# Second norms of blocks 1 and 2 on GpSimd, a 5120-column product, first loads in pieces, and a new order

## The chip, the core and the metric

The kernel runs on one core of a Trainium2 chip. The metric is the device time of one execution in microseconds, and the time of a kernel is the median of several executions. Of the kernel before there are three: 256.29, 257.15 and 257.36 us, median 257.15 us. A further execution was recorded by the hardware profiler; it took 256.16 us, and its span from the first to the last instruction is 254.4 us.

The names of the engines in the profile: PE is TensorE (matmuls, transposes), PEld its weight load, DVE is VectorE, ACT is ScalarE, POOL is GpSimd, SP is the engine that issues most DMAs. A "q" behind a name is the engine's sequencer.

## The reference, cut to what matters

Sequence length 2048, width 640, hidden width 1728, bfloat16. Part A is a gated long convolution: a four-tap shift of `k`, times `v`, convolved over the sequence with a filter as long as the sequence (through a Fourier transform), times the normed query. Part B is a SwiGLU layer behind a second norm.

```
h  = x + A(layernorm(x), k, v, shift_k, ssm_k, ssm_D)
h2 = h + B(layernorm(h), w_gate, w_up, w_down)

A: kv = shift4(k, shift_k) * v
   y  = irfft(rfft(kv, 4096) * rfft(ssm_k, 4096))[:2048] + kv * ssm_D
   return q * y
B: return (silu(x @ w_gate) * (x @ w_up)) @ w_down
```

## The kernel before

The sequence is cut into four blocks of 512 rows (`NB` = 4, `BLK` = 512). A row tile of a block is 128 partitions by four rows `r` by 640 columns. For each block j the work is staged, and the stage names stand in the program:

- `g`: the filter piece `ssm_k` is transposed on PE (line 431) and evicted from PSUM (line 435); block 3 uses DMA transposes instead. In block 0 a row of `ssm_D` is added (line 437).
- `k`: the shifted `k` by small matmuls with the diagonal taps `diag` (line 570, "conv" below), times `v`, gives `kv` (line 578, straight out of PSUM on DVE, or line 579 on ACT and line 580 on DVE). Block 0 first transposes `k` on PE (line 533) into `T` (line 537).
- `G`, `X`: the spectra of `g` and `kv`, matmuls with the basis `WF` (line 352), evicted by line 344 (ACT) or line 345 (DVE), and some sums (lines 377 to 409). In block 0 the spectra and the products are made in two half-widths of 320 columns (`CUTS`).
- `m`: products of spectra, A = sum of X[i] times H[j-i] (function `mac`): the first pair of a block by line 591, the others by lines 612 (product) and 615 (sum into A). A whole-width product has 2560 columns, a half-width one 1280. Function `sum_into` lets a sum go either on DVE or as an accumulating DMA that POOL issues (line 256).
- `n`, `i`: `ln1` takes the sums of x (lines 671 and 628 on ACT) and the first norm; `inverse` forms the inverse transform (DVE lines 697 to 733, PE line 745), multiplies it by the normed query (lines 685 or 682, then line 759), adds x (line 762) and takes the second norm of h.
- `t`: h is scaled (lines 685 or 682) and transposed: in block 0 on PE (line 783, evicted by line 785), in blocks 1 to 3 by DMA transposes (line 776).
- `f`: the SwiGLU layer: line 846 (up and gate, 540 matmuls of 512 columns), lines 835 and 837 (evictions), line 840 (product), lines 915 and 900 (down projection), line 924 (out of PSUM) or lines 933 and 935 (last block).

The FFN of block j is written behind the mixing of block j+1, so that PE can do the one while the other engines prepare the other.

A norm turns four sums per partition into a scale and a bias. On DVE it is `norm`: nine or ten instructions of 128 by 4 elements, with a polynomial for the inverse root (lines 643 to 653). On GpSimd it is `apart`: five instructions with a power (lines 660 to 664). Before the change the first norms of blocks 1 to 3 run in `apart`, everything else in `norm`.

Nothing schedules itself: every step is an operation with an engine, a function and its buffers, and the list `ORDER` of operation numbers says in which order they are issued; a negative number takes the operation's other engine (ACT or DVE for evictions, DVE or a DMA for sums, the SP or the POOL queue for loads). Each engine takes its instructions in that order, so an instruction that waits holds up everything behind it on its engine. Buffers are handed out along the same list: 13 large tiles `big`, eight spectra `S`, five rows `row`, four PSUM tiles `ps` that all PE results share.

PSUM tiles are the tightest: PE may be at most four results ahead of the engines that evict them.

Of the kernel before, what the change touches and what calls it, by code (L numbers as in the profile page):

```python
# [14 lines left out]
ALU = mybir.AluOpType  # L15

S_TOT = 2048
D = 640
FF = 1728
P = 128  # L20
# [18 lines left out]
GPIECES = ((0, KT),)  # L39
# [150 lines left out]
def kernel(ctx: ExitStack, tc: tile.TileContext, A_q, A_k, A_v, A_shift_k, A_ssm_k, A_ssm_D, B_x,  # L190
# [156 lines left out]
    def forward(src, c, rs, ps, ws, first, last, holds):  # L347

        def mm():
            for i, r in enumerate(rs):  # L350
                for h in ws:
                    nc.tensor.matmul(ap(ps)[:, h, 0:NH], ap(WF)[:, c, r, :], ap(src)[:, r, h * NH:(h + 1) * NH],  # L352
                                     start=(first and i == 0), stop=(last and i == len(rs) - 1), skip_group_check=True)
        pe(136 * len(ws) * len(rs), mm, [(src, r) for r in rs] + [WF] + ([] if first else [ps]), [ps], holds)
# [152 lines left out]
    def load_k(j):  # L507

        if j == 0:
            return load_t(kk, 0)  # L510
# [593 lines left out]
```

## Time and profile before

| | value |
|---|---|
| three executions | 256.29, 257.15, 257.36 us; median 257.15 us |
| the profiled execution | 256.16 us, of which the span is 254.4 us |
| DMA traffic | 41.04 MB in 51906 packets, mean 161 GB/s |
| POOL, ACT busy | 67.4 us (27%), 174.9 us (69%) |
| granted TensorE clock, mean | 0.993 |

The page gives busy time by engine, the span in 40 slices with a digit for the busy share of each engine, the chain that ended last, and groups of instructions by source line. Queries of the trace give the same by window, by engine in order of time, and the waits. In a row of the timeline the first number is the start in us from the span's start, the second the length of that row, "xN" the number of instructions merged in it, and the bracket the idle time just before it with what ended it. Instructions that follow each other are pipelined, so a row's busy time per instruction is longer than the step from one start to the next; sums below use the step. The start of a matmul is exact, its end is modelled.

### The profile page before, as it was taken

What the parts mean: (1) busy time and instruction counts of PE and PEld (TensorE: products, weight loads), DVE (VectorE), ACT (ScalarE), POOL (GpSimd) and SP (SyncE); (2) the same over time, 40 slices, a digit from 0 to 9 for tenths busy, and PEclk for the clock granted to TensorE, in tenths of its full rate; (3) what the DMA queues carried; (4) which work ended last, traced back from release to release, by engine and by line L of the source; (5) the groups of instructions that cost most, each with busy time, mean ns of one, the idle gap of its engine ahead of it and who ended that gap; (6) DMA issues with size and microseconds to landing.
All of it is one profiled execution on the core that took longest, in us unless ns stands there. A gap on an engine that the chain in (4) does not pass through costs nothing.

```text
span 254.4 us, 5139 instructions
## 1 busy us (share of the span) xinstructions
PE 246.7 (97%) x2070; PEld 145.2 (57%) x2070; DVE 192.1 (76%) x280; ACT 174.9 (69%) x306; POOL 67.4 (27%) x73
## 2 busy tenths in 40 slices
PE   8699999999999999999999999999999999999994
PEld 7566667744555576645554567544447744444663
DVE  0599999999989999999979999999998300102213
ACT  3969999998679899686788984348668144635200
POOL 6300020113444011149932013136920024000000
PEclk9799999999999999999999999999999999999999
DMA  6999777998897979898976386989973229000011
GB/s 239 350 356 234 196 203 141 211 249 199 159 330 199 176 169 183 205 200 207 278 142 119 83 126 119 187 192 212 211 158 80 58 46 131 0 0 0 3 41 62
DMA packets 51906, 41.04 MB, mean 161 GB/s; under 512 B 25461, under 2 KB 46202, under 8 KB 51882
## 3 DMA queue, kind: packets, MB, share of 16 engines
q1 hardware_dynamic: 45040, 26.94, 41.5%
q0 software_dynamic: 6832, 13.77, 30.5%
q8 instruction: 16, 0.26, 0.4%
q14 instruction: 8, 0.07, 0.1%
q10 hardware_dynamic: 10, 0.01, 0.0%
HBM read 22.03 MB, written 4.59 MB: 105 GB/s over the span
## 4 chain that ended last, share of the span: by engine, by line
PE 86%; ACT 6%; DMA 3%; DVE 2%; issue 1%; SPq 0%; DVEq 0%
PE ps L846 46%; PE ps L915 22%; PE ps L352 7%; ACT S L344 5%; PE ps L745 4%; PE ps L570 4%; DMA big<-in_A_ssm_k_dram 3%; PE ps L431 1%; PE ps L900 1%; DVE big L578 1%; ACT big L435 1%; ACT row L628 1%; DVE S L345 1%; ACT row L685 0%; ACT big L785 0%
## 5 line engine op out<-in xcount | busy, mean ns | idle before, releaser
L846 PE MATMUL ps<-big,big 128*128 128x512 bf16 x540 | 120.6, 379 | 0.0
L846 PEld LDWEIGHTS <-big 128*128 128x128 bf16 x540 | 52.0, 98 | 60.1 <-issue 0.5
L915 PE MATMUL ps<-wd,tT 128*128 128x320 bf16 (+2 forms) x416 | 59.5, 299 | 0.0
L915 PEld LDWEIGHTS <-tT 128*128 128x128 bf16 x416 | 40.3, 98 | 16.8 <-issue 1.3
L352 PE MATMUL ps<-big,WF 128*128 128x320 bf16 x224 | 37.0, 298 | 1.1 <-ACT S L344 0.4
L344 ACT ACTIVATE S<-ps 128x640 bf16<-128x640 f32 (+1 forms) x62 | 33.4, 620 | 4.3 <-PE ps L352 4.0
L612 DVE TENSOR_TENSOR big<-S,S 128x2560 bf16<-128x2560 bf16 x24 | 34.8, 1486 | 0.7 <-DMA S<-big 0.4
L835 ACT CAST co<-ps 128x1024 bf16<-128x1024 f32 x24 | 24.1, 1016 | 15.3 <-PE ps L846 15.1
L837 ACT ACTIVATE tT<-ps 128x1024 bf16<-128x1024 f32 x24 | 24.6, 1024 | 13.8 <-PE ps L846 13.7
L352 PEld LDWEIGHTS <-WF 128*128 128x128 bf16 x224 | 21.4, 97 | 12.7 <-issue 3.2
L628 ACT ACTIVATE row<-big 128x640 bf16<-128x640 bf16 x32 | 23.8, 752 | 2.2 <-DVE big L762 1.2
L840 DVE TENSOR_TENSOR tT<-tT,co 128x2048 bf16<-128x2048 bf16 x12 | 14.7, 1222 | 13.0 <-ACT co L835 9.0
L615 DVE TENSOR_TENSOR S<-S,big 128x2560 bf16<-128x2560 bf16 x16 | 23.4, 1486 | 0.1
L256 POOL DMA_DIRECT2D S<-big x9 | 10.9, 1210 | 46.0 <-DVE big L612 14.6
L685 ACT ACTIVATE row<-big,sm 128x640 bf16<-128x640 bf16 x22 | 19.6, 928 | 2.7 <-DVE sm L653 1.7
L858 DVE TENSOR_TENSOR tT<-tT,co 128x512 bf16<-128x512 bf16 x4 | 1.7, 422 | 21.7 <-ACT tT L856 21.3
L925 POOL DMA_DIRECT2D out_dram<-row x12 | 12.1, 1314 | 17.3 <-ACT row L924 17.2
L256 POOL DMA_DIRECT2D S<-S x4 | 5.7, 1431 | 38.2 <-ACT S L344 38.2
L924 ACT CAST row<-ps 128x640 bf16<-128x640 f32 x12 | 8.1, 690 | 10.3 <-PE ps L900 6.6
L759 DVE SCALAR_TENSOR_TENSOR row<-row,ps 128x640 bf16<-128x640 bf16 x16 | 12.8, 818 | 3.1 <-PE ps L745 2.9
L570 PEld LDWEIGHTS <-T 64*128 64x128 bf16 x640 | 12.0, 113 | 4.2 <-issue 4.0
L570 PE MATMUL ps<-diag,T 64*128 64x64 bf16 x640 | 13.5, 198 | 0.0
(93 smaller groups left out, 276.1 us busy)
## 6 DMA issues: line engine op xcount, KB each, us to landing
S<-big POOLq DMA_DIRECT2D x9, 640.0 KB, 6.3
big<-in_B_w_gate_dram SPq DMA_DIRECT2D x11, 320.0 KB, 5.6
big<-in_B_w_up_dram SPq DMA_DIRECT2D x10, 320.0 KB, 6.6
big<-in_A_q_dram SPq DMA_DIRECT2D x4, 640.0 KB, 5.5
big<-in_A_ssm_k_dram SPq DMA_DIRECT2D x4, 640.0 KB, 7.0
big<-in_A_v_dram SPq DMA_DIRECT2D x4, 640.0 KB, 4.3
S<-S POOLq DMA_DIRECT2D x4, 640.0 KB, 6.8
wd<-in_B_w_down_dram SPq DMA_DIRECT2D x1, 2080.0 KB, 12.2
```

Of the source, the lines that this page charges most:

```text
L256: nc.gpsimd.dma_start(out=to(), in_=what(), accum_op=ALU.add, max_dma_last_dim=2 * D * 2)
L344: plan.add("act", 700 if n else 430, lambda: nc.scalar.activation(dst(), src(), ACT.Copy, scale=by), [ps], [part], (), ("dve", 820 if n el ...
L352: nc.tensor.matmul(ap(ps)[:, h, 0:NH], ap(WF)[:, c, r, :], ap(src)[:, r, h * NH:(h + 1) * NH], start=(first and i == 0), stop=(last and i ...
L570: nc.tensor.matmul(out()[:, b, c, :], k, ap(diag)[at, c, t, :], start=(t == 0), stop=(t == 3))
L612: dve(1490, lambda b=b, xs=xs, hs=hs: nc.vector.tensor_mul(flat2(b), X.part(xs), H.part(hs)), [X.at(xs), H.at(hs)], [b], [A.b])
L615: f(A.part(dst), A.part(dst), flat2(b))
L628: act(825, lambda r=r, junk=junk: nc.scalar.activation(ap(junk), ap(x)[:, r, :], ACT.Square, scale=D ** -0.5, accum_out=sm(s, 1)[:, r:r + ...
L685: nc.scalar.activation(ap(row), ap(x)[:, r, :], ACT.Identity, bias=sm(s, 5)[:, r:r + 1], scale=sm(s, 4)[:, r:r + 1])
L835: act(1010, lambda ps=ps: nc.scalar.copy(ap(co)[:, at:at + 2, :], ap(ps)), src, [(co, gi % 2)])
L837: act(1010, lambda ps=ps: nc.scalar.activation(ap(tT)[:, c:c + 2, :], ap(ps), ACT.Silu), src, [done(range(c, c + 2), ROWS)])
L846: nc.tensor.matmul(ap(ps)[:, i, :], ap(w)[:, k, off:off + P], ap(hT)[:, k, :], start=(k == 0), stop=(k == KT - 1))
L915: nc.tensor.matmul(ap(ps)[:, hf, 0:n], ap(tT)[:, c, at:at + P], ap(wd)[:, c, col:col + n], start=j % 2 == 0 and c == order[0], stop=j % 2 ...
```

## The change

Five things change in the text of the program.

1. The second norms of blocks 1 and 2 (`FAR`) go to `apart` on GpSimd, which gains two instructions for the mean: seven instead of ten on DVE.
2. In `mac`, the first two products of a block, X's first half with both halves of H, become one instruction of 5120 columns: X's half is read twice (a broadcast) and H in turned order. Only whole-width products do so, in blocks 1, 2 and 3; block 0 keeps half-widths.
3. The first loads of `k` and `v` come in two halves each, `WF` in two halves, the first filter piece in two pieces (two and three of five 128-row groups).
4. The matmuls of a spectrum wait for their half of `WF`, the transposes for their piece of the filter.
5. `ORDER` is new throughout. With it some sums change engine: 11 instead of 13 large and 4 instead of 6 small sums are accumulating DMAs, the rest are on DVE. Ahead of the first FFN matmul PE has 148 instead of 160 matmuls of line 352; the total is the same.

```diff
@@ constants
-GPIECES = ((0, KT),)
+FAR = (1, 2)
+GPIECES = ((0, 2), (2, KT))
...
 ORDER = [
-    0, 4, 2, 15, 1, 16, 5, 6, 19, 22, 20, 24, 26, 17, 18, 3, 23, 344, 9, 7, -26, -11, 28, -15, 353, 44, 29, 12, 200, 13,
+    0, 15, 1, 16, 2, 9, 4, 17, 5, 3, 6, 23, 22, 7, 24, 26, 21, 19, 28, 11, 14, 32, 20, -14, 29, 30, -34, -11, -32, 12, 18,
...
@@ forward
-        pe(136 * len(ws) * len(rs), mm, [(src, r) for r in rs] + [WF] + ([] if first else [ps]), [ps], holds)
+        pe(136 * len(ws) * len(rs), mm, [(src, r) for r in rs] + [(WF, c // 2)] + ([] if first else [ps]), [ps], holds)
...
@@ class Spec
+        def turns(self, swapped=False):
+            t = ap(self.b).rearrange("p a (s b) d -> p a s (b d)", s=2)
+            return t if self.swapped == swapped else t[:, :, ::-1, :]
+
+        def twice(self, sin):
+            t = self.part(sin)
+            return t.unsqueeze(2).broadcast_to([P, 2, 2, 2 * D])
...
@@ load_k
-            return load_t(kk, 0)
+            return load_t(kk, 0, 2)
...
@@ mac
-            dve(n, op(v.tensor_mul, of(A, 0), of(X, 0), of(H, 0)), [x0, H.at(0, ws)], [A.at(0, ws)])
-            dve(n, op(v.tensor_mul, of(A, 1), of(X, 0), of(H, 1)), [x0, H.at(1, ws)], [A.at(1, ws)])
+            if len(ws) == 2:
+                dve(2820, op(v.tensor_mul, lambda: A.turns(H.swapped), lambda: X.twice(0), lambda: H.turns(H.swapped)),
+                    [x0, H.at(0), H.at(1)], [A.at(0), A.at(1)])
+            else:
+                dve(n, op(v.tensor_mul, of(A, 0), of(X, 0), of(H, 0)), [x0, H.at(0, ws)], [A.at(0, ws)])
+                dve(n, op(v.tensor_mul, of(A, 1), of(X, 0), of(H, 1)), [x0, H.at(1, ws)], [A.at(1, ws)])
...
@@ apart
-    def apart(s):
+    def apart(s, mean=None, rs=range(R)):
...
         def go():
+            if mean:
+                v.tensor_scalar(sm(s, 2), sm(s, 0), -1.0 / D, None, op0=ALU.mult)
+                v.tensor_add(sm(s, 2), sm(s, 2), sm(mean, 2))
...
-        plan.add("pool", 5500, go, [root], [s])
+        plan.add("pool", 7000 if mean else 5500, go, [root] + ([mean] if mean else []), [s])
...
@@ inverse
-            norm(s, n1, rs)
+            (apart if plan.block in FAR else norm)(s, n1, rs)
...
@@ first loads
-    v = load_t(vv, 0)
+    v = load_t(vv, 0, 2)
...
-    load(P * R * 4 * P * 2, 4096, lambda: nc.sync.dma_start(out=ap(WF), in_=wf_h.ap()), [WF])
+    for c in (0, 2):
+        load(P * R * 2 * P * 2, 2048, lambda c=c: nc.sync.dma_start(out=ap(WF)[:, c:c + 2], in_=wf_h.ap()[:, c:c + 2]), [(WF, c // 2)])
```

The new program's lines stand 1 to 17 further down; where both are named, the line of before comes first: conv 570/579, transposes of g 431/432, forward 352/353, its evictions 344/345 and 345/346, kv 578/587, the second norm's DVE instructions 643/656 and up, FFN 846/862.

**First place: the loads and PE's first real work.** On SP, the queue of the loads at the program's start, before (big_72 is `k`, big_73 the query x, big_74 the filter piece g, big_75 `v`):

```order
L317 DMA big_72<-in_A_k_dram 128x2560
L323 DMA big_73<-in_A_q_dram 128x2560
L309 DMA big_74<-in_A_ssm_k_dram 128x5x512
L317 DMA big_75<-in_A_v_dram 128x2560
L987 DMA WF<-const_wf 128x2048
L807 DMA big_76<-in_B_w_up_dram 128x5x256
```

And the same stretch of SP's queue after the change:

```order
L318 DMA big_72<-in_A_k_dram 128x1280 x2
L324 DMA big_73<-in_A_q_dram 128x2560
L310 DMA big_74<-in_A_ssm_k_dram 128x3x512
L310 DMA big_74<-in_A_ssm_k_dram 128x2x512
L1004 DMA WF<-const_wf 128x1024
L318 DMA big_75<-in_A_v_dram 128x1280
L1004 DMA WF<-const_wf 128x1024
L318 DMA big_75<-in_A_v_dram 128x1280
```

The same bytes go in the same order as far as g; behind it the halves of `WF` and `v` take turns, and the FFN weights that came next have moved back. On PE, the transposes of `k` (line 533/542) end and the following work begins; before, the transposes of g come first:

```order
L533 MATMUL ps_96<-ident,big_72 128x128
L431 LDWEIGHTS big_74
L431 MATMUL ps_94<-ident,big_74 128x128
...
L570 LDWEIGHTS T
L570 MATMUL ps_93<-diag,T 128x64
```

After, the first 40 matmuls of the conv stand there, and g's transposes (line 432) behind them:

```order
L542 LDWEIGHTS big_72
L542 MATMUL ps_94<-ident,big_72 128x128
L579 LDWEIGHTS T
L579 MATMUL ps_93<-diag,T 128x64
...
L432 LDWEIGHTS big_74
```

So PE's first work behind the transposes of `k` no longer needs g, but needs `T`, which is made from those transposes, and the taps `diag`.

**Second place: DVE ahead of block 1's spectrum.** The second norm of block 0 (sm_99) stays on DVE in both; `kv` of block 1 (lines 578/587 and 580/589) stands among it. Before:

```order
L643 SCALAR_TENSOR_TENSOR sm_99<-sm_99,sm_98 128x4
L580 TENSOR_TENSOR big_72<-big_72,big_74 128x640
L578 TENSOR_TENSOR big_72<-ps_93,big_74 128x2x5x64
L578 TENSOR_TENSOR big_72<-ps_94,big_74 128x2x5x64
L645 TENSOR_TENSOR sm_99<-sm_99 128x4
L435 COPY big_79<-ps_96 128x640
L646 SCALAR_TENSOR_TENSOR sm_99<-sm_99 128x4
```

After:

```order
L656 SCALAR_TENSOR_TENSOR sm_99<-sm_99,sm_98 128x4
L778 TENSOR_TENSOR big_73<-big_73,row_90 128x640
L658 TENSOR_TENSOR sm_99<-sm_99 128x4
L587 TENSOR_TENSOR big_75<-ps_96,big_81 128x2x5x64
L589 TENSOR_TENSOR big_75<-big_75,big_81 128x640
L436 COPY big_79<-ps_93 128x640
L659 SCALAR_TENSOR_TENSOR sm_99<-sm_99 128x4
L660 TENSOR_SCALAR sm_99<-sm_99 128x4
L661 TENSOR_TENSOR sm_99<-sm_99 128x4
L587 TENSOR_TENSOR big_75<-ps_94,big_81 128x2x5x64
L662 SCALAR_TENSOR_TENSOR sm_99<-sm_99 128x4
L589 TENSOR_TENSOR big_75<-big_75,big_81 128x640
```

The last of block 1's four kv rows has moved back behind four more instructions of the norm.

**Third place: POOL and ACT at block 1's second norm (sm_101).** On POOL the seven instructions stand between two accumulating DMAs (line 257, sums of spectra):

```order
L257 DMA S_67<-S_70 128x2x1280
L674 TENSOR_SCALAR sm_101<-sm_101 128x4
L675 TENSOR_TENSOR sm_101<-sm_101,sm_100 128x4
L676 TENSOR_TENSOR sm_101<-sm_101 128x4
L677 TENSOR_TENSOR sm_101<-sm_101 128x4
L678 TENSOR_SCALAR sm_101<-sm_101 128x4
L679 TENSOR_TENSOR sm_101<-sm_101,root 128x4
L680 TENSOR_TENSOR sm_101<-sm_101 128x4
L257 DMA S_71<-big_80 128x2x1280
```

On ACT, which scales h with the result (line 701), a run of evictions stands between the last sum of squares (line 641) and the first row that needs the norm:

```order
L641 ACTIVATE row_87,sm_101<-big_82 128x640
L345 ACTIVATE S_66<-ps_93 128x640
L851 CAST co_92<-ps_95 128x1024
...
L345 ACTIVATE big_83<-ps_93 128x640
L345 ACTIVATE big_83<-ps_95 128x640
L701 ACTIVATE row_90<-big_82,sm_101 128x640
L345 ACTIVATE big_79<-ps_93 128x640
```

Before, DVE made this norm, spread over its other work; now ACT's first scaling waits for POOL, and the evictions behind it wait with it.

78 rows, old and new, of the table ORDER are left out of this document.

## The prediction

> **What bounds the kernel now.** First the page: busy shares, and two rows of its slices (40 equal slices of 6.4 us, a digit is tenths of busy time).
>
> ```profile
> span 254.4 us, 5139 instructions
> PE 246.7 (97%) x2070; PEld 145.2 (57%) x2070; DVE 192.1 (76%) x280; ACT 174.9 (69%) x306; POOL 67.4 (27%) x73
> PE   8699999999999999999999999999999999999994
> DVE  0599999999989999999979999999998300102213
> ```
>
> PE is full from the fourth slice to the last. So other engines matter only where PE waits for them. Next, then, PE's timeline at the front and at the last block's FFN.
>
> ```profile
> 6.51 0.44 PE L533 MATMUL ps<-ident,big 128*128 128x128 bf16 x5 [0.20 <-ACT T L537]
> 8.78 0.52 PE L431 MATMUL ps<-ident,big 128*128 128x128 bf16 x5 [1.83 <-DMA big<-in_A_ssm_k_dram]
> 16.48 0.76 PE L570 MATMUL ps<-diag,T 64*128 64x64 bf16 x40
> 45.19 0.44 PE L783 MATMUL ps<-ident,row 128*128 128x128 bf16 x5
> 45.46 0.71 PE L352 MATMUL ps<-big,WF 128*128 128x320 bf16 x4
> 47.83 4.00 PE L352 MATMUL ps<-big,WF 128*128 128x320 bf16 x28
> 51.72 8.58 PE L846 MATMUL ps<-big,big 128*128 128x512 bf16 x39
> 206.81 29.31 PE L846 MATMUL ps<-big,big 128*128 128x512 bf16 x135
> ```
>
> The only long wait is 1.83 us, for the first filter piece. What I take as the hinge is 51.72, the start of the first FFN matmul: before it PE does what the front's chain allows, behind it PE never waits as long as the others keep up. The rest is 254.4 − 51.72 = 202.7 us of PE work. I therefore forecast the hinge and the rest apart.
>
> **The rest.** Twelve matmuls of line 352 move behind the hinge. Their step is (51.72 − 47.83)/28 = 0.139 us, so the rest becomes 202.7 + 12 × 0.139 = 204.4, if nothing new stalls PE.
>
> **The front, step by step.** DVE carries it. Its rows, with the filter's DMA (from the chain of waits) and POOL's `diag`:
>
> ```profile
> 1.72 7.02 DMA big<-in_A_ssm_k_dram
> 3.78 5.12 POOL L978 TENSOR_SCALAR diag<-row,taps 128x64 bf16<-128x64 bf16 x12 [1.26 <-DVE taps L970]
> 9.34 0.49 DVE L435 COPY big<-ps 128x640 bf16<-128x640 bf16 x1 [1.11 <-PE ps L431]
> 12.65 0.47 DVE L437 TENSOR_TENSOR big<-big,row 1x640 bf16<-1x640 bf16 x1
> 13.05 0.47 DVE L435 COPY big<-ps 128x640 bf16<-128x640 bf16 x1
> 13.45 1.53 DVE L578 TENSOR_TENSOR big<-ps,big 128x640 bf16<-128x640 f32 x2
> 21.13 0.82 DVE L591 TENSOR_TENSOR S<-S,S 128x1280 bf16<-128x1280 bf16 x1
> 40.36 0.16 DVE L643 SCALAR_TENSOR_TENSOR sm<-sm,sm 128x4 f32<-128x4 f32 x1
> 42.30 0.15 DVE L645 TENSOR_TENSOR sm<-sm 128x4 f32<-128x4 f32 x1
> 42.96 0.17 DVE L647 TENSOR_SCALAR sm<-sm 128x4 int32<-128x4 int32 x1
> 44.14 0.16 DVE L653 TENSOR_TENSOR sm<-sm 128x4 f32<-128x4 f32 x1
> 48.85 1.48 DVE L591 TENSOR_TENSOR S<-S,S 128x2560 bf16<-128x2560 bf16 x1
> 50.25 1.48 DVE L591 TENSOR_TENSOR big<-S,S 128x2560 bf16<-128x2560 bf16 x1
> ```
>
> 1. *g lands at the same time.* It came at 1.72 + 7.02 = 8.74. The bytes ahead of it in SP's queue are the same; four issues instead of three stand there. I take 8.75 ± 0.4. Its transposes are no longer PE's first work: the conv runs from about 7.95 (POOL makes eight `diag` pieces, 3.78 + 8 × 5.12/12 = 7.2; DVE's last `T` is ready by 7.8) to 8.7, in what was the idle stretch. First eviction of g on DVE 9.2, before 9.34.
> 2. *Four evictions and the row add follow.* At DVE's step of 13.05 − 12.65 = 0.40 they end at 9.2 + 5 × 0.40 = 11.25; before it was 13.45, since convs stood between the transposes.
> 3. *The clock may fall or not.* The windows (PE busy is the second number, the granted clock the one ahead of the DMA share):
>
> ```profile
> 2.24:5.65 3.41, 3.23 (x34) 2.96 (x32) 0.18 (x1) 0.63 (x2) 2.15 (x6) 1.00 0.93 356
> 5.65:9.07 3.42, 1.39 (x21) 1.10 (x19) 2.14 (x11) 2.78 (x7) 3.25 (x8) 1.00 0.99 326
> 9.07:12.48 3.41, 3.41 (x73) 2.99 (x72) 1.22 (x3) 3.41 (x11) 0.00 (x0) 0.50 1.06 368
> ```
>
>    A window in which PE was busy 1.39 of 3.42 us was followed by one at clock 0.50, one with 3.23 by full clock. After the change the conv fills the middle window to some 55%, between the two. If the clock falls, half of PE's 3.41 us is lost, most of it behind the four PSUM tiles: 0 to 0.5 us on the end. I take 0.3.
> 4. *To the first product.* Before, 21.13 − 13.45 = 7.7. After the change one conv of 0.76 (row at 16.48) and 0.25 of DVE work are left over for it: + 1.0. First product at 11.25 + 7.7 + 1.0 = 19.95, 1.2 earlier.
> 5. *The products and the inverse.* Before 40.36 − 21.13 = 19.2, DVE nearly without a gap. The same 18 half-width instructions stand there; an `h` row (0.40), a kv sum (0.40) and three norm instructions (about 0.5 together) move out, and I add 0.2 of waits: 18.1, so 38.05.
> 6. *To block 1's last kv row.* By the order list after the change: two products straight out of PSUM (half of the 1.53 at 13.45 each), four instructions of 640 columns at 0.40, and six norm instructions at (44.14 − 42.96)/6 = 0.20: 1.5 + 1.6 + 1.2 = 4.3, so 42.35; before, the last row was done at 42.30. Here the lead is given back, because norm instructions now stand ahead of it.
> 7. *From there PE is the limit*: 36 matmuls at 0.139 and 25 transposes at (45.46 − 45.19)/5 = 0.054 are 6.4. Hinge 42.35 + 6.4 + 0.3 (step 3) = 49.05 against 51.72.
>
> Sum: 49.05 + 204.4 = 253.45, 0.95 under 254.4. The profiled execution took 256.16, 1.76 more than its span; the median of the runs, 257.15, lies 0.99 above that. So 253.45 + 1.76 + 0.99 = **256.2 us**.
>
> **The other edits.** *DVE's total*: 20 norm instructions of 0.20 go, 4.0 us. Two large sums at 50.25 − 48.85 = 1.40 and two small ones at 0.40 come back from DMAs, 3.6. DVE gains almost nothing, and PE does not wait for it in the middle anyway.
>
> *The 5120-column product* does not stand in the trace. These groups bound it:
>
> ```profile
> L591 DVE TENSOR_TENSOR S<-S,S 128x2560 bf16<-128x2560 bf16 x6 | 8.9, 1486 | 0.0
> L591 DVE TENSOR_TENSOR S<-S,S 128x1280 bf16<-128x1280 bf16 x4 | 3.2, 821 | 0.0
> L733 DVE TENSOR_TENSOR S<-big 128x1280 bf16<-128x1280 bf16 x6 | 4.7, 818 | 0.0
> ```
>
> The line through 1280 and 2560 columns has 0.52 ns per column, so 5120 take 1486 + 2560 × 0.52 = 2.82 us, against 2 × 1.40 of step: nothing gained. Line 733 reads its operand in turned order at the plain rate, so I take 2.82. The upper end is half rate for a repeated operand, 5.6.
>
> *The second norms on GpSimd.* The trace has first norms there, first and last instruction of each of two:
>
> ```profile
> 66.85 0.50 POOL L660 TENSOR_TENSOR sm<-sm 128x4 f32<-128x4 f32 x1 [5.33 <-ACT row L671]
> 72.46 0.54 POOL L664 TENSOR_TENSOR sm<-sm 128x4 f32<-128x4 f32 x1
> 114.03 7.09 POOL L660 TENSOR_TENSOR sm<-sm 128x4 f32<-128x4 f32 x1 [1.79 <-ACT row L671]
> 124.93 0.21 POOL L664 TENSOR_TENSOR sm<-sm 128x4 f32<-128x4 f32 x1
> ```
>
> Five instructions took 72.46 + 0.54 − 66.85 = 6.15 us and 11.11 us. Seven at those rates are 8.6 to 15.6; the first is the more usual make-up (no single instruction of 7 us in it), and I take 10 to 11. It hides behind ACT's evictions between the last sum of squares and the first scaling of h: nine of them for block 1. In the trace ACT's evictions at that place run at PE's pace:
>
> ```profile
> 81.71 0.70 ACT L344 ACTIVATE S<-ps 128x640 bf16<-128x640 f32 x1
> 94.69 2.20 ACT L344 ACTIVATE big<-ps 128x640 bf16<-128x640 f32 x3
> ```
>
> Eleven of them from 81.71 to 96.9, 1.38 us each; eight such steps are 11 us of cover. So the norm just fits, and costs nothing at 11 us or less. Beyond that ACT's scaling stands at the head of its queue with the evictions behind it, PE has four PSUM tiles, some 1.5 us, and then stops; POOL's accumulating DMAs behind the norm come late too.
>
> Here a rule speaks against the change. One instruction of 128 by 4 elements took 7.09 us while DVE ran two-input instructions without a gap, others about 1.45, DVE's step. The Trainium skill, page "SBUF — State Buffer", section "Who interferes with whom", says that DVE and GpSimd share a pair of ports as an exclusive lock, held for a whole instruction, and that a DVE instruction with two SBUF inputs contends with a GpSimd one that reads SBUF. The trace agrees with these two numbers; by that rule a 5120-column product holds GpSimd off twice as long.
>
> **The rivals.**
> - *The front's whole lead is kept.* The 1.0 in step 4 and some 0.7 of DVE waits in step 5 are guesses from the order list; DVE had gaps of that size before. Without them the hinge is 47.35: 256.2 − 1.7 = **254.5**. Against it: step 6 shows the same norm in DVE's way.
> - *The lead is lost at the last block.* These rows end DVE's and SP's part of block 3:
>
> ```profile
> 198.94 0.16 DVE L653 TENSOR_TENSOR sm<-sm 128x4 f32<-128x4 f32 x1
> 199.49 5.17 SPq L776 DMA_TRANSPOSE big<-row  x4
> ```
>
>   The last transpose is issued at 199.49 + 5.17 = 204.66 and its data is needed at 206.81: about 2 us for the transfer. If PE comes 0.95 us sooner and DVE, whose work is the same within 0.4 us, doesn't, PE waits there for most of it: 256.2 + 0.8 = **257.0**, no change.
> - *Slower: a norm on GpSimd outlasts its cover.* At 15.6 us against 11 the scaling is 4.6 late, less 1.5 that PE holds: 3 us in one block, 256.2 + 3 = **259.2**; in both, 262. It decides from 11 us on. For it speaks the row of 7.09, against it the row at 66.85.
> - *Slower: the 5120-column product at half rate.* 3 × 2.8 = 8.4 us more on DVE, a part of it covered by DVE's 24% of idle time: **260 to 265**. Line 733's row speaks against it.
> - *The change doesn't do what it says*, the conv can't start before g because `diag` or `T` is late: PE idles as before and the time of before stays, **257.2**; I count it with the case of no change.
>
> **How the numbers follow.** The forecast, 256.2, has chance 0.40, own range 255.2 to 257.2; the front's whole lead 0.24; lost at the last block (or not brought) 0.19; the norm late 0.13; half rate 0.04. 0.5%, about what a measurement of this kernel can tell from no change, is 1.29 us: faster means under 255.86. Faster: 0.24 + 0.17 of the forecast's (its range lies across the bound) = 0.41. Same: 0.23 + 0.19 = 0.42. Slower: 0.17. For the range, 253.6 (the kept lead less 0.9) to 259.4 (one late norm and a little) leaves out the half-rate case, the case of two late norms and the tails.
>
> **What would show it.** Right: line 432's first transpose at about 8.75 behind a conv, the first half-width product near 19.95, the last kv row of block 1 near 42.35, the first FFN matmul near 49, PE without a wait behind it; a group of 5120 columns with a mean near 2.82 us; GpSimd's seven instructions in 8.6 to 11 us. Wrong: PE waiting in front of a line 353 or 862 for ACT (a late norm), PE waiting for a DMA at the last block's FFN (lost there), a 5120 row of over 4 us, or g landing later than 9.2, which moves every step behind it.

## The result and the profile after

The changed kernel is slower. Five runs gave 258.44 to 261.66 us, median 260.56, beside a median of 257.36 us for the kernel before (five runs); the ratio is 1.0119, 95% interval 1.0087 to 1.0151. The forecast was 256.2 us, in a range that ended at 259.4. The profiled execution took 258.87 us with a span of 257.2, 2.8 more than the span before. The ratios here and below leave out executions more than 1.5% above the fastest of their kernel, the medians don't, so runs are compared by their ratios, of which 1% is 2.6 us.

These lines of the page answer to those of before: span, busy shares, and PE's and DVE's slices.

```profile
span 257.2 us, 5111 instructions
PE 244.4 (95%) x2053; PEld 145.1 (56%) x2070; DVE 194.6 (76%) x264; ACT 174.4 (68%) x306; POOL 82.0 (32%) x80
PE   8699799999979999999989999999999999999995
DVE  3589999999996999999859999999998500031213
```

PE's row has a 7 in the twelfth slice (70.7 to 77.2 us) and an 8 in the 21st (128.6 to 135), where before it had nines; the 7 in the fifth belongs to the front. So the loss lies in two places behind the front. PE's timeline shows them, and the start of the first FFN matmul above them:

```profile
49.79 7.72 PE L862 MATMUL ps<-big,big 128*128 128x512 bf16 x34
75.56 0.43 PE L353 MATMUL ps<-big,WF 128*128 128x320 bf16 x2 [0.92 <-ACT S L345]
77.28 1.24 PE L862 MATMUL ps<-big,big 128*128 128x512 bf16 x5 [0.74 <-ACT tT L853]
129.21 0.87 PE L579 MATMUL ps<-diag,T 64*128 64x64 bf16 x40 [0.72 <-ACT tT L853]
130.60 0.38 PE L862 MATMUL ps<-big,big 128*128 128x512 bf16 x1 [0.52 <-ACT big L588]
```

The hinge came 1.93 us earlier (51.72 before). The rest is 257.2 − 49.79 = 207.4 us where 204.4 was forecast, 3.0 too much, and the four waits in brackets sum to 0.92 + 0.74 + 0.72 + 0.52 = 2.9. All four are waits for ACT's evictions. ACT's timeline just ahead of each pair says what ACT was doing:

```profile
70.09 1.03 ACT L853 ACTIVATE tT<-ps 128x1024 bf16<-128x1024 f32 x1
73.19 1.73 ACT L701 ACTIVATE row<-big,sm 128x640 bf16<-128x640 bf16 x2 [2.07 <-POOL sm L680]
74.83 0.68 ACT L345 ACTIVATE S<-ps 128x640 bf16<-128x640 f32 x1
123.96 0.70 ACT L588 CAST big<-ps 128x640 bf16<-128x640 f32 x1
127.33 0.92 ACT L701 ACTIVATE row<-big,sm 128x640 bf16<-128x640 bf16 x1 [2.67 <-POOL sm L680]
128.15 1.00 ACT L853 ACTIVATE tT<-ps 128x1024 bf16<-128x1024 f32 x1
```

ACT stood at the first scaling of x (line 701, 685 before) until GpSimd's last norm instruction (line 680), with evictions behind it. This is the **first** norm of blocks 1 and 2, which was on GpSimd before the change too, not the second one that the change moves there. GpSimd's and DVE's timelines in block 1 show why it was late (the two engines apart):

```profile
62.30 5.94 POOL L676 TENSOR_TENSOR sm<-sm 128x4 f32<-128x4 f32 x1 [2.84 <-ACT row L687]
68.31 1.45 POOL L677 TENSOR_TENSOR sm<-sm 128x4 f32<-128x4 f32 x1
72.62 0.54 POOL L680 TENSOR_TENSOR sm<-sm 128x4 f32<-128x4 f32 x1
...
62.08 1.48 DVE L628 TENSOR_TENSOR S<-S,big 128x2560 bf16<-128x2560 bf16 x1
63.48 1.48 DVE L625 TENSOR_TENSOR big<-S,S 128x2560 bf16<-128x2560 bf16 x1
64.89 1.48 DVE L628 TENSOR_TENSOR S<-S,big 128x2560 bf16<-128x2560 bf16 x1
66.29 0.48 DVE L589 TENSOR_TENSOR big<-big,big 128x640 bf16<-128x640 bf16 x1
66.69 1.48 DVE L628 TENSOR_TENSOR S<-S,big 128x2560 bf16<-128x2560 bf16 x1
68.21 1.49 DVE L713 TENSOR_TENSOR big<-S 128x2560 bf16<-128x2560 bf16 x1
```

GpSimd had its sums at 62.30. Its first instruction, 128 by 4 elements, ended at 68.24, just where DVE's stream has its first gap behind 62.30: the sum at 66.69 ends at 68.17, and line 713, which needs that sum, starts at 68.21. The steps before are 1.40 us or 0.40, with each instruction starting before the last one ends. In block 2 the same instruction took 7.73 us:

```profile
115.31 7.73 POOL L676 TENSOR_TENSOR sm<-sm 128x4 f32<-128x4 f32 x1 [2.73 <-ACT row L687]
```

Why this cost nothing before is seen in ACT's first scalings of x in the kernel before, block 1 and block 2:

```profile
74.79 2.54 ACT L685 ACTIVATE row<-big,sm 128x640 bf16<-128x640 bf16 x3
125.17 1.74 ACT L685 ACTIVATE row<-big,sm 128x640 bf16<-128x640 bf16 x2 [1.07 <-POOL sm L664]
```

In block 1 the sums came at 66.85, the norm ended at 73.00, and ACT reached its first scaling at 74.79. After the change the sums come 4.5 us earlier, the norm ends at 73.16 all the same, and ACT reaches the scaling at 71.1. The new order counts on a norm that follows its sums; the norm follows DVE's gaps. In block 2 ACT already waited 1.07 us before the change, and PE didn't feel it. There the sums now come 1.3 us later (115.31 for 114.03), the first instruction takes 7.73 us instead of 7.09, and ACT waits 2.67.

The second norms were on time. Their first and last instruction in block 1, and ACT's first scaling of h:

```profile
83.35 1.40 POOL L674 TENSOR_SCALAR sm<-sm 128x4 f32<-128x4 f32 x1 [0.95 <-DVE row L775]
91.11 1.81 POOL L680 TENSOR_TENSOR sm<-sm 128x4 f32<-128x4 f32 x1
96.80 0.92 ACT L701 ACTIVATE row<-big,sm 128x640 bf16<-128x640 bf16 x1
```

They took 9.6 us in block 1 (and 8.3 in block 2), and ACT came to the result 3.9 us after it was there, with no wait.

### The profile page after: what moved, and what is told of

Read it like the earlier page. It is cut to its first block, busy times and chain, and to the rows that moved or that the text cites. A ratio compares the mean times of both kernels' runs of the same rounds, so it can differ in the third digit from the quotient of the medians.

```text
span 257.2 us, 5111 instructions
## 1 busy us (share of the span) xinstructions
PE 244.4 (95%) x2053; PEld 145.1 (56%) x2070; DVE 194.6 (76%) x264; ACT 174.4 (68%) x306; POOL 82.0 (32%) x80
## 4 chain that ended last, share of the span: by engine, by line
PE 63%; DVE 17%; DMA 5%; ACT 5%; POOL 5%; issue 3%; SPq 1%; ACTq 0%; DVEq 0%; POOLq 0%
PE ps L862 31%; PE ps L931 22%; PE ps L353 4%; DVE S L600 4%; POOL sm L676 3%; DMA big<-in_A_ssm_k_dram 3%; DMA S<-big 2%; DVE big L600 2%; PE ps L761 2%; PE ps L579 2%; DVE big L713 1%; DVE S L628 1%; DVE S L716 1%; PE ps L916 1%; ACT S L345 1%
## 5 line engine op out<-in xcount | busy, mean ns | idle before, releaser
L862 PE MATMUL ps<-big,big 128*128 128x512 bf16 x523 | 118.8, 379 | 2.7 <-issue 0.8
L353 PE MATMUL ps<-big,WF 128*128 128x320 bf16 x224 | 37.7, 302 | 2.5 <-ACT big L436 1.6
L851 ACT CAST co<-ps 128x1024 bf16<-128x1024 f32 x24 | 24.2, 1014 | 10.4 <-PE ps L862 10.2
L628 DVE TENSOR_TENSOR S<-S,big 128x2560 bf16<-128x2560 bf16 x18 | 26.4, 1483 | 0.5 <-DMA S<-big 0.4
L701 ACT ACTIVATE row<-big,sm 128x640 bf16<-128x640 bf16 x24 | 21.8, 933 | 4.7 <-POOL sm L680 4.7
L941 POOL DMA_DIRECT2D out_dram<-row x12 | 11.0, 1102 | 43.0 <-ACT row L940 19.4
L676 POOL TENSOR_TENSOR sm<-sm 128x4 f32<-128x4 f32 x5 | 16.0, 3209 | 5.7 <-ACT row L687 5.6
L257 POOL DMA_DIRECT2D S<-big x7 | 9.3, 1327 | 24.9 <-DVE S L600 19.4
```

The lines of the kernel that those rows point to most:

```text
L628: f(A.part(dst), A.part(dst), flat2(b))
L676: v.tensor_mul(sm(s, 6), sm(s, 2), sm(s, 2))
L701: nc.scalar.activation(ap(row), ap(x)[:, r, :], ACT.Identity, bias=sm(s, 5)[:, r:r + 1], scale=sm(s, 4)[:, r:r + 1])
L851: act(1010, lambda ps=ps: nc.scalar.copy(ap(co)[:, at:at + 2, :], ap(ps)), src, [(co, gi % 2)])
L862: nc.tensor.matmul(ap(ps)[:, i, :], ap(w)[:, k, off:off + P], ap(hT)[:, k, :], start=(k == 0), stop=(k == KT - 1))
```

## The experiments

The first four runs were made to tell three theories apart: (1) ACT waits for the first norms, which DVE's gapless stream holds up; (2) DVE's product for the SwiGLU layer (line 856) comes too late in the new order, since in block 1 it ends at 76.1, just ahead of PE's second wait; (3) the second norms outlast their cover in the runs that were not profiled. Ratios are to the kernel before, timed on the same chip.

**The changed kernel again** (no edit).

> The changed kernel once more, for its spread (258.44 to 261.66 us so far) and for a second profile. Theory 1 (ACT's first scalings of x wait for the first norm on GpSimd, whose instructions come through only where DVE's stream has a gap): ACT waits for the norm's last instruction in front of line 701 in blocks 1 and 2, by 2 to 4 us each, and a slower execution shows longer waits there. Theory 2 (DVE's product for the SwiGLU layer, line 856, comes too late in the new order): PE waits in front of line 862 behind that product. Theory 3 (the second norms outlast their cover): ACT waits in front of line 701 of h for the seven instructions. Median 260 to 261 by all.

Measured: median 259.54 us, ratio 1.0100 (1.0057 to 1.0144). In the profile the same two stretches: ACT waited 4.8 us in all for line 680, 2.8 at the longest, and PE 0.9, 0.8, 0.7 and 0.5 us behind it. The loss is reproducible, and in the same place.

**Without the wait.** The scalings take a constant, and the norm is computed all the same.

```diff
-                applied(x, n1, r, t, (), True)
+                applied(x, fake if plan.block in (1, 2) else n1, r, t, (), True)
```

> The scaling of x in blocks 1 and 2 takes a constant scale and bias instead of the first norm (the result of the norm is left out there; GpSimd still computes it). Theory 1: ACT's waits of 2.1 and 2.7 us go, and the time falls by about 3 us, to 257.0 to 258.0. Theory 2: block 1 keeps its loss of about 1.7 us, since line 856 still ends at about 76.1; the time falls by 1.5 at most, to 259. Theory 3: no change, 260.5.

Measured: median 256.60 us, ratio 0.9996 (0.9971 to 1.0021), about 2.7 us below the changed kernel by the ratios and a little below what theory 1 gave. GpSimd's first instruction still took 5.94 and 7.72 us. Theories 2 and 3 fall: line 856 and the second norms stand in the order where they did.

The four waits of PE are gone, but two others of 0.9 us in all stand in block 2. The late norm still holds up what is behind it in GpSimd's queue, a load of FFN weights and an accumulating DMA of h (line 257):

```profile
125.11 1.59 POOL L823 DMA_DIRECT2D big<-in_B_w_up_dram  x1
126.03 1.60 POOL L257 DMA_DIRECT2D big<-row  x1
133.39 1.25 PE L862 MATMUL ps<-big,big 128*128 128x512 bf16 x5 [0.39 <-DMA big<-in_B_w_up_dram]
135.37 3.40 PE L862 MATMUL ps<-big,big 128*128 128x512 bf16 x15 [0.46 <-ACT co L851]
```

The second of them is for an eviction that stands behind ACT's wait of 1.65 us for that accumulating DMA. In the next run, where the norm itself is early, ACT waits 0.19 us there and PE not at all. So the late norm has a second, smaller way to PE, through GpSimd's own queue.

**Gaps for GpSimd.** Four sums move up on DVE, each directly behind the product that it waits for; no other engine's order changes. On DVE in block 1 (block 2 alike, with big_84 and big_80):

```diff
 L625 TENSOR_TENSOR big_81<-S_68,S_64 128x2560
+L628 TENSOR_TENSOR S_71<-S_71,big_81 128x2x1280
 L625 TENSOR_TENSOR big_80<-S_68,S_64 128x2560
-L628 TENSOR_TENSOR S_71<-S_71,big_81 128x2x1280
+L628 TENSOR_TENSOR S_71<-S_71,big_80 128x2x1280
 L625 TENSOR_TENSOR big_79<-S_68,S_64 128x2560
-L628 TENSOR_TENSOR S_71<-S_71,big_80 128x2x1280
```

> Four of DVE's sums of spectra are moved up directly behind the product that they need, so that DVE's stream has a gap after every pair; DVE's work and all other engines' orders stay. Theory 1: the first norm of block 1 gets its first instruction through at about 63.5 instead of 68.2 and ends 3 to 4 us earlier, that of block 2 ends 2 to 3 us earlier, and the time falls by 2 to 3 us, to 257.5 to 258.5. Theory 2 and theory 3: within 0.5 us of the changed kernel.

Measured: median 255.48 us, ratio 0.9951 (0.9923 to 0.9979): about 3.8 us below the changed kernel by the ratios, more than theory 1 gave, and 0.5% faster than the kernel before. GpSimd's norm of block 1 and the DVE rows beside it:

```profile
61.72 1.46 POOL L676 TENSOR_TENSOR sm<-sm 128x4 f32<-128x4 f32 x1 [2.84 <-ACT row L687]
67.43 0.47 POOL L680 TENSOR_TENSOR sm<-sm 128x4 f32<-128x4 f32 x1
...
61.63 1.49 DVE L625 TENSOR_TENSOR big<-S,S 128x2560 bf16<-128x2560 bf16 x1
63.15 1.49 DVE L628 TENSOR_TENSOR S<-S,big 128x2560 bf16<-128x2560 bf16 x1
```

The first instruction ended at 63.18, with the sum that waited for its product starting at 63.15 (a step of 1.52 instead of 1.40). The norm took 6.2 us instead of 10.9. In this profile nothing on ACT waits for line 680, and the span of 253.4 with the hinge at 49.21 leaves a rest of 204.2 us, the 204.4 of the forecast.

**The second norms back on DVE** (`FAR = ()`), ten instructions in a row where GpSimd's stood.

> The second norms of blocks 1 and 2 are on DVE again, ten instructions in a row where GpSimd's stood in the order; all else as changed. Theory 3: the loss goes, 257 to 258. Theory 1 and theory 2: the first norms and line 856 are where they were; DVE has 4 us more, of which little is on the path: 260 to 261.5.

Measured: median 261.36 us, ratio 1.0182 (1.0158 to 1.0207), slower than the changed kernel by some 2 us by the ratios. DVE's chain to block 2's inverse is later by the norm's time (line 713 starts 1.9 us later, counted from GpSimd's first norm in block 1); GpSimd's first norm of block 2 waited 9.58 us for its gap instead of 7.73, and ACT 4.6 us for it. So undoing the part I had suspected makes it worse, through the same wait.

**The other way out: ACT's order.** The evictions go ahead of the scaling that waits. In block 1 (in block 2 one eviction of line 853 goes ahead of the first scaling):

```diff
 L853 ACTIVATE tT_85<-ps_94 128x1024
+L345 ACTIVATE S_66<-ps_93 128x640
+L853 ACTIVATE tT_85<-ps_95 128x1024
 L701 ACTIVATE row_90<-big_82,sm_100 128x640
 L701 ACTIVATE row_87<-big_82,sm_100 128x640
-L345 ACTIVATE S_66<-ps_93 128x640
 L701 ACTIVATE row_89<-big_82,sm_100 128x640
-L853 ACTIVATE tT_85<-ps_95 128x1024
```

> The changed kernel, with ACT's first scalings of x (line 701) moved behind one eviction of a spectrum and one of the SwiGLU layer in block 1, and behind one of the SwiGLU layer in block 2; DVE's, GpSimd's and PE's orders stay. The first norms still wait 5.9 and 7.7 us for their first instruction and end where they did. If the loss is that ACT stands at a scaling with evictions behind it, PE's waits of 1.6 us in block 1 and most of the 1.2 us in block 2 go, and the time falls by 2 to 3 us, to 257 to 258. If the late norm itself holds the inverse up, PE waits for line 775's results instead, and the time stays at 259.5 to 260.5.

Measured: median 256.44 us, ratio 1.0001 (0.9972 to 1.0029), about 2.5 us below the changed kernel by the ratios (on another chip). The norm was as late as ever (first instruction 5.94 and 7.70 us), ACT waited 0.4 us for it, and PE's waits for lines 345 and 853 are gone from its list of waits (0.5 and 0.4 us for lines 588 and 851 are left). So the late norm by itself costs little; what costs most is that evictions queue behind it.

**The kernel before with such gaps.** Two pairs of product and sum ahead of block 2's inverse; on DVE:

```diff
 L612 TENSOR_TENSOR big_72<-S_66,S_64 128x2560
-L612 TENSOR_TENSOR big_82<-S_66,S_64 128x2560
 L615 TENSOR_TENSOR S_71<-S_71,big_72 128x2x1280
 L498 TENSOR_TENSOR S_70<-big_73,S_70 128x1280
+L612 TENSOR_TENSOR big_82<-S_66,S_64 128x2560
 L615 TENSOR_TENSOR S_71<-S_71,big_82 128x2x1280
```

> The kernel before, with two pairs of product and sum put side by side on DVE ahead of block 2's inverse, so that the first norm on GpSimd gets through at about 117.5 instead of 121. PE waits nowhere behind the front in the kernel before, so by theory 1 nothing changes: within 0.5 us of before, though ACT's wait of 1.07 us for the norm goes. If the sums' new place is worth something by itself, this run is faster by 1 us or more.

Measured: median 256.62 us, ratio 0.9999 (0.9967 to 1.0030). ACT's wait of 1.07 us for the norm is gone, and the time is that of before: where PE doesn't feel the norm, gaps gain nothing, which speaks for the wait, and not the sums' new place, as what r1_gaps gained. The control isn't clean, though. In its profiled execution (258.32 us, one of the longest) PE waited 1.53 us in block 3 for ACT (line 671), which the kernel before doesn't show; whether the other executions have this wait isn't known.

**The parts of the change, on top of the gaps.** First the long product, undone in all three blocks:

```diff
-L600 TENSOR_TENSOR S_71<-S_65,S_69 128x5120
+L600 TENSOR_TENSOR S_71<-S_65,S_69 128x2x1280 x2
```

> The changed kernel with the sums moved up (as in r1_gaps), and the product of 5120 columns again two of 2560. If the long product costs what the line through the shorter ones says, 2.82 us against 2.81 in steps, the time stays that of r1_gaps, 255.5 within 0.6. If its length holds GpSimd off where it matters, this run is faster by 0.5 or more. In the trace two rows of 2560 columns, together 2.8 us.

Measured: median 254.86 us, ratio 0.9906 (0.9878 to 0.9935). Then the second norms:

```diff
-FAR = (1, 2)
+FAR = ()
```

> The changed kernel with the sums moved up, and the second norms of blocks 1 and 2 on DVE, ten instructions in a row. If the move to GpSimd gains nothing (the prediction: PE doesn't wait for DVE in the middle), 255.5 within 0.6. If DVE's two microseconds a block delay the next block's chain, which r1_second_norms_dve suggests (the first norm of block 2 waited 9.58 us instead of 7.73), 256 to 257.

Measured: median 256.39 us, ratio 0.9961 (0.9935 to 0.9987). The profiled execution took 509.43 us, so its trace isn't read. Then the filter's pieces:

```diff
-L310 DMA big_74<-in_A_ssm_k_dram 128x3x512
-L310 DMA big_74<-in_A_ssm_k_dram 128x2x512
+L310 DMA big_74<-in_A_ssm_k_dram 128x5x512
```

> The changed kernel with the sums moved up, and the first filter piece loaded by one DMA instead of two. If the two pieces matter, the transposes of g start later, at 9.5 to 10, and the first FFN matmul starts 0.3 to 0.6 us later: 255.8 to 256.2. If the load's end is set by the bytes ahead of it alone, no change: 255.5.

Measured: median 256.75 us, ratio 0.9972 (0.9936 to 1.0009). These three stood on one chip, r1_gaps on another, so their ratios are compared. All three intervals overlap that of r1_gaps (0.9923 to 0.9979): no part is shown to gain or lose by itself, and none of the three expectations is decided. The ratios lean against the long product (some 1.2 us less without it) and hardly for the other two parts (0.3 us more without the second norms' move, 0.5 more without the pieces). The version with gaps and two products is the fastest of the study by its ratio and its median.

The long product was undone without the gaps as well, by the same edit:

> The changed kernel with the product of 5120 columns as two of 2560, the sums where the change has them. If the long product has no part in the loss, the first norms' first instructions wait 5.9 and 7.7 us as before and the time stays at 259.5 to 260.5. If it has, those waits shorten and the time falls by 1 us or more.

Measured: median 258.60 us, ratio 1.0063 (1.0025 to 1.0102), and the first norms' first instructions took 6.01 and 7.80 us. The product has no part in the wait. That it costs some 1 us elsewhere is possible by both pairs of ratios (0.4% each) and shown by neither.

**What lets GpSimd through.** A small DVE instruction with one input and no dependency stands between two long ones:

```diff
             if op.fn:
                 op.fn()
+            if op.n in (281, 505):
+                nc.vector.tensor_scalar(ap(spare), ap(root), 1.0, None, op0=ALU.mult)
```

> The changed kernel with two more instructions on DVE, 128 by 4 elements with one input in SBUF and no dependency on their neighbours: one between the sum at 62.1 and the product at 63.5 of block 1, one behind the product at 116.6 of block 2. If GpSimd comes through wherever DVE's stream of long two-input instructions is broken, its first instruction ends at about 63.6 and 118.1 and the time falls by 3 to 4 us, to 255.5 to 257. If only a gap behind a dependent pair lets it through, the first instruction still takes 5.9 and 7.7 us and the time stays at 259.5 to 260.5.

Measured: median 258.25 us, ratio 1.0029 (0.9983 to 1.0075). The profiled execution took 263.46 us, so only the sequence is read from it; GpSimd, then DVE, in block 1:

```profile
61.60 1.35 POOL L676 TENSOR_TENSOR sm<-sm 128x4 f32<-128x4 f32 x1 [2.84 <-ACT row L687]
63.02 4.60 POOL L677 TENSOR_TENSOR sm<-sm 128x4 f32<-128x4 f32 x1
...
62.79 0.18 DVE L1092 TENSOR_SCALAR spare<-root 128x4 f32<-128x4 f32 x1
62.88 1.48 DVE L625 TENSOR_TENSOR big<-S,S 128x2560 bf16<-128x2560 bf16 x1
67.60 1.49 DVE L713 TENSOR_TENSOR big<-S 128x2560 bf16<-128x2560 bf16 x1
```

The first instruction came through at the small one, and then the second waited, from 63.02 to 67.62, for the gap ahead of line 713. In block 2 it went the same way: the first instruction took 2.80 us, the second 4.93. Neither expectation was right: the break lets one instruction through, not the norm. The norm's end hardly moves (10.2 us from its start in block 1, for 10.9), and the median lies between the two expectations; the interval overlaps that of the changed kernel, so a gain isn't shown.

The last edit puts a one-input copy at the head of the first norms:

```diff
+            else: v.tensor_scalar(sm(s, 7), sm(s, 2), 1.0, None, op0=ALU.mult)
             v.tensor_mul(sm(s, 6), sm(s, 2), sm(s, 2))
```

> The changed kernel with one instruction more at the head of the first norms on GpSimd: a copy by tensor_scalar, one input, as the second norms begin with. In the traces the second norms' first instruction came through at DVE's next boundary, the first norms' first (two inputs) didn't. If the kind of the first instruction decides, the norms of blocks 1 and 2 end 4 us earlier and the time falls to 256 to 257. If not, the copy takes the long wait in its place, and the time stays at 259.5 to 261.

Measured: median 260.59 us, ratio 1.0171 (1.0097 to 1.0246). The added copy took the long wait, 5.95 and 7.76 us. So it doesn't matter for the wait whether GpSimd's first instruction has one input or two.

## Why the prediction was wrong, step by step

- *g at 8.75*: 9.48 and 10.17 for its two pieces in the profile (the last DMA took 7.47 us from 2.66). The first eviction came at 10.52, not 9.2. This was the largest miss in the front, and the prediction had named it as a sign of being wrong (later than 9.2); in the other profiles with two pieces the first transposes started between 8.1 and 9.3.
- *Evictions and row add, 2.0 us*: 10.52 to 12.52, as forecast (the prediction's sum is 11.2, not 11.25).
- *The clock, 0 to 0.5, taken as 0.3*: its part isn't separated. After the window in which PE was busy 1.69 of 3.42 us the clock fell in part:

```profile
5.65:9.07 3.42, 1.69 (x51) 1.27 (x48) 1.55 (x7) 2.18 (x5) 1.75 (x4) 1.00 0.98 317
9.07:12.48 3.41, 2.53 (x60) 2.18 (x60) 1.96 (x5) 2.96 (x10) 0.00 (x0) 0.90 1.04 379
12.48:15.89 3.41, 3.41 (x57) 2.11 (x52) 2.80 (x6) 1.98 (x8) 0.00 (x0) 0.60 1.03 384
```

  From 12.52 to the first product took 9.1 us where 8.7 was forecast. In the profile of r2_gaps_two_products, with PE busy 2.95 us in the second of these windows, the clock didn't fall at all. There the runs with a mean granted clock of 0.993 took 254.91 and 255.33 us and those with 1.0 253.86 and 254.22, about 1.1 us apart; in r1_gaps the two kinds hardly differ.
- *First product 19.95*: 21.61. *From there to the second norm of block 0, 18.1 us*: 17.6 (39.25). *To the last kv row, 4.3*: 3.85 (43.10). *PE's 6.4 behind it*: 6.7. The hinge came at 49.79, forecast 49.05: the front was right in its mechanism and 0.7 us off. That it came so near is in part luck: the first eviction of g was 1.3 us late and the steps behind the first product 0.9 us shorter than forecast, and in the other profiles with two pieces (the one of 509.43 us left out) the hinge lay anywhere from 47.83 to 49.41.
- *The rest, "204.4, if nothing new stalls PE"*: **this is the step that failed.** It put the wait for the first norms at nothing. The rest measured 207.4, by PE's four waits for ACT in blocks 1 and 2 (2.9 us); in r1_gaps, where they are gone, 204.2. In r1_no_wait and r4_late_scaling it was 205.1, each with 0.9 us of waits of PE left. The condition was checked for the edits that the diff names and not for the places where the new order lets ACT reach a norm's result sooner. The row at 114.03, 7.09 us for one instruction, lay in the prediction and already showed that a norm's end can be set by DVE's gaps; I used it for the price of a norm that is new on GpSimd, and not for the ones that stood there. The prediction also took this row as agreeing with a lock held for one instruction. It doesn't: DVE's instructions there last at most 1.48 us, and five of them started during the wait.
- *A norm on GpSimd outlasts its cover (0.13)*: the right mechanism, ACT's scaling at the head of its queue with evictions behind it and PE out of PSUM tiles, on the wrong norm. The second norms took 8.3 and 9.6 us, under the 10 to 11 that I took, and in block 1 the result was there 3.9 us before ACT came for it. The price of 3 us that the rival gave, 259.2, is near what the profiled execution lost, by luck: it was worked out for another norm, in one block.
- *The lead lost at the last block*: no. It was lost in blocks 1 and 2.
- *The 5120-column product, 2.82 us*: 2818 ns in the groups. It does hold a GpSimd instruction that meets it: the last one of block 1's second norm (line 680) took 2.63 us in r1_gaps, during this product, and 0.81 in r2_gaps_two_products. ACT came for the result later in both, so that cost nothing. *DVE's total, 4.0 us less of norms and 3.6 more of sums*: DVE was busy 194.6 us instead of 192.1, and behind the front PE waited for none of it.

The median of 260.56 lies 1.7 us above the profiled execution of the same kernel, and the changed kernel's runs spread over 3.2 us. These five runs all had a mean granted clock of 0.993, so the clock's mean doesn't explain it. What the longer of them lost was not profiled and stays open.

## What to carry to other kernels

When an order is made anew, every wait for GpSimd is new, even where nothing was moved there: ask for each result of it what DVE runs between its inputs and its consumer, and where the first gap in that stream is. Ask too what stands behind it in GpSimd's own queue. A consumer in a queue with PSUM evictions should stand behind them, or the producer should get its gaps; each of the two edits moved only four instructions and took 2.5 to 3.8 us off here. And the condition under which a sum holds ("if nothing stalls") has to be gone through place by place for each engine whose order changed, not for the lines of the diff.

## What the runs showed of the hardware

- A GpSimd instruction of 128 by 4 elements that starts while DVE runs two-input instructions without a gap can wait through several of them: 5.94 us past four starts of DVE instructions, 7.73 past six, 9.58 past seven (r1_second_norms_dve). In these three it came through at the first pair on DVE of which the second waits for the end of the first (a step of 1.52 us instead of 1.40). Two sums into the same spectrum in a row, 1.40 us from start to start (117.96 in the changed kernel), didn't let it through. In r3_tiny_one_input it came through at one small instruction with a single input. DVE's steps during the long waits were 1.40 us, as elsewhere.
- The Trainium skill, page "SBUF — State Buffer", section "Who interferes with whom", says that the shared ports are held for the whole instruction and that a DVE instruction with at most one SBUF input doesn't contend, outside the modes that use both ports. Of the first the runs show more: the wait does not end with the instruction that runs. For the second r3_tiny_one_input is no test: no run shows in which mode the small instruction ran, and it may have let GpSimd through by its length alone.
- This is not the whole rule. In r1_gaps the second and third instruction of the norm (ends at 64.70 and 66.14) came through at starts of DVE instructions at 64.56 and 65.97, with ordinary steps of 1.41 us and no gap. What decides it there no run here shows.
